# Last products moved into the next phase, and clamps, differences and low weight parts moved from GpSimd to VectorE, in a retention and double feed-forward kernel

## The chip, the cores and the metric

One core of a Trainium2 chip. The metric is the device time of one execution in microseconds, the median of several runs. The program is written with its order by hand: nothing is reordered afterwards, and each engine works through its own instructions in that order.

## The reference

The input passes through a causal retention and then two feed-forward stages, with T = 4608 tokens and a width of 512:

```python
scores = scale * (q @ k.T)                 # 64 (batch, head) pairs of 576 x 64
x = (scores * decay) @ v                   # -> x, 4608 x 512
h = x @ w_in                               # 512 -> 2048
x2 = (h * cos(h)) @ w_out                  # 2048 -> 512
z = max(x2 @ w1, x2 @ w2, x2 @ w3)         # 512 -> 768 each
out = z @ w_out2                           # 768 -> 512
```

All arrays are float32.

## The kernel before

Every large product is made of 2x2 quarters by a scheme with seven products in place of eight (A11, A12, A22, S1 to S4, `P_A11` and so on). Sums and differences of quarters are formed ahead of the products: of the weights in `sums`, of the activations in `difference`, which forms T1 to T4 (T1 and T3 are the two halves of the tile `ta`, T2 and T4 those of `tb`). For precision each operand is split in a high and a low part: ScalarE casts the high part, and VectorE or GpSimd subtracts it from the value to give the low part (`low`, `pair_low`, `piece_low`). One term of a product is three matmuls of 128x128 by 256 columns (low by high, high by high, high by low).

The tokens stand in nine blocks of 512. The program has five phases on TensorE:

1. **A**: the retention of all blocks (units of two heads, `att_unit`) and, beside it, `x @ w_in` for the first half of w_in (tiles `w_wi`, `d_a`, `b_a`, `a_a`, input `x_x`). 18 groups of seven products (`group_in`).
2. **B**: the second half of w_in, with `x_x` read back from memory as `x_y`. 18 groups.
3. **wo**: `g @ w_out` (tiles `w_wo`; the gated `g` is read back as `k_g` and split into `x_g`, `h_g`, `l_g` by `build_out`). 36 groups of seven products (`phase_out`).
4. **b**: the three branches (tiles `w_b`, input `x_z`). 45 groups.
5. **o**: the last product (tiles `w_o`, input `h_m`, `l_m`). 18 groups.

**Slots.** The order is made with an agenda: `at(n, fn)` puts a step n slots ahead, and `tick()` runs the steps that are due. One slot stands for one product, 12 matmuls with two weight pairs. A step that is put late by number of slots is behind those products in every engine's order, not later by a clock.

**The last product of a group.** The product P_A22 of a `group_in` group accumulates onto its bank `d` after S3 has been read from it by VectorE (`plus`, L403). It is held back in `pending` and made by `last_product` (L390) four products into the next group. At the end of phase B and of phase b there is no next group, and `last_product()` stands by itself (L851, L923).

**The gate** h * cos(h) of phases A and B is made per half group by `gate` (L436): ScalarE rounds to whole turns (L441), VectorE forms the rest (L445), GpSimd clamps it (L446), ScalarE takes the cosine (L450), VectorE multiplies (L453), and the result goes to memory.

**Weights.** Outside the phases that need them they are brought to float32 quarters by `background` (widen, join and total; then sums, high and low parts, the low ones on GpSimd by L216) and stored; `take_split` loads the quarters of `wi` 4 to 7 and of `wo`, sums and splits them on VectorE (L190 to L193, L212, L216) just ahead of their use. All `x` tiles share 22 buffers, all weight tiles 8.

The lines that set the order around the change are these:

```python
for i, n in enumerate((-27, -22, -18, -14)):
    at(endA + n, lambda i=i: take_split("wi", 4 + i, 0))
at(offs[0], lambda: difference(o, 1, nc.gpsimd))
at(offs[0], lambda: difference(o, 3, nc.gpsimd))
at(1, turns); at(2, rest); at(4, cosine); at(5, times)
```

Of the kernel before, what the change touches and what calls it, by code (L numbers as in the profile page):

```python
# [101 lines left out]
def retention_ffn(ctx: ExitStack, tc: tile.TileContext, att, w_in, w_out, w123, w_out2, cst, out):  # L102
# [119 lines left out]
    def background(kind, i, arena):  # L222
# [33 lines left out]
        def low(k):  # L256
            piece_low(k, st["src", k], st["p", k], nc.gpsimd)
# [132 lines left out]
    def last_product():  # L390
# [5 lines left out]
        tick()  # L396
# [39 lines left out]
    def gate(s, name, dst):  # L436
# [297 lines left out]
    def build_out(name, n, src, offs, load):  # L734
# [24 lines left out]
        at(offs[0], lambda: difference(o, 1, nc.gpsimd))  # L759
        at(offs[0], lambda: difference(o, 3, nc.gpsimd))  # L760
# [57 lines left out]
    def phase_out(kind, groups, todo, xs, scale, dsts):  # L818
        for j, k in todo:
# [31 lines left out]
    last_product()  # L851

# [128 lines left out]
```

## Time and profile before

| | us |
|---|---|
| median of 3 runs | 1563.21 (1559.2 to 1564.91) |
| the profiled execution's own time | 1566.85 |
| its span from first to last instruction | 1565.0 |
| TensorE busy / VectorE / ScalarE / GpSimd | 1468.8 / 1233.1 / 728.8 / 493.4 |
| mean granted TensorE clock | 0.98 of full |

The shares of the span are 94%, 79%, 47% and 32%. Matmuls are pipelined, so a busy TensorE is not one at its best pace. What counts is how many matmuls a stretch holds beside its length, and what ended the waits within it. An engine's lines give its instructions in groups: how many, busy time in all, mean of one in ns, and the idle time before them with what ended it.

### The profile page before, as it was taken

How to read it: one execution, taken by the hardware profiler on the slowest of the kernel's cores; microseconds unless marked ns; L12 is line 12 of the kernel's file. 1: busy time of each engine (PE TensorE's matmuls, PEld its weight loads, DVE VectorE, ACT ScalarE, POOL GpSimd, SP SyncE). 2: the span in 40 equal slices, each digit the busy share in tenths (PEclk: the TensorE clock that was granted, in tenths of full speed). 3: DMA queues.
4: the chain of work that ended last, by engine and by line, in shares of the span. 5: the costliest groups of instructions: out<-in, count | busy, mean ns of one | idle time of the engine just before them, and what ended most of it. 6: DMA issues, size and time to landing. Idle time of an engine off the chain costs nothing. (4 is left out here: it accounts for less than half of the span.)

```text
span 1565.0 us, 30902 instructions
## 1 busy us (share of the span) xinstructions
PE 1468.8 (94%) x12506; PEld 1424.4 (91%) x12506; DVE 1233.1 (79%) x1611; ACT 728.8 (47%) x1214; POOL 493.4 (32%) x364
## 2 busy tenths in 40 slices
PE   7799999997998996899999999999999999998998
PEld 5698989996988996899999999899999999998998
DVE  6988989898878869899999999746554554538997
ACT  4465655565666665344443444434433333323332
POOL 3544444434333334455444445201110000003221
PEclk9999999997999997999999999999999999999999
DMA  7588888875998873545556656944332211153543
GB/s 287 202 307 316 313 295 301 304 256 212 330 339 303 326 276 132 183 165 177 191 188 209 206 168 253 390 176 142 129 100 83 68 46 50 68 193 137 176 164 133
DMA packets 83086, 324.47 MB, mean 207 GB/s; under 512 B 9216, under 2 KB 9216, under 8 KB 76928
## 3 DMA queue, kind: packets, MB, share of 16 engines
q1 hardware_dynamic: 82944, 322.51, 58.0%
q8 instruction: 98, 1.61, 0.4%
q14 instruction: 44, 0.36, 0.1%
HBM read 190.35 MB, written 132.12 MB: 206 GB/s over the span
## 5 line engine op out<-in xcount | busy, mean ns | idle before, releaser
L781 PE MATMUL wo<-h_g,w_wo 128*128 128x256 f32 x1728 | 317.9, 285 | 0.0
L781 PEld LDWEIGHTS wo<-h_g,w_wo 128*128 128x128 f32 x1728 | 273.0, 194 | 0.0
L781 PE MATMUL wo<-l_g,w_wo 128*128 128x256 f32 x864 | 250.3, 290 | 20.7 <-DVE l_g L754 20.1
L379 PE MATMUL d_b<-x_z,w_b 128*128 128x256 f32 x1944 | 250.1, 284 | 7.0 <-DVE s_b L403 4.9
L379 PEld LDWEIGHTS d_b<-x_z,w_b 128*128 128x128 f32 x1944 | 241.2, 193 | 7.9 <-DVE s_b L403 5.1
L781 PEld LDWEIGHTS wo<-l_g,w_wo 128*128 128x128 f32 x864 | 167.6, 194 | 27.3 <-DVE l_g L754 27.0
L446 POOL TENSOR_SCALAR t_a<-t_a 128x1024 f32<-128x1024 f32 x72 | 91.9, 1281 | 179.9 <-DVE t_a L445 138.2
L379 PE MATMUL d_a<-x_x,w_wi 128*128 128x256 f32 x864 | 126.1, 298 | 9.3 <-DVE x_x L358 7.4
L379 PE MATMUL b_b<-x_z,w_b 128*128 128x256 f32 x972 | 131.9, 284 | 2.0 <-DVE x_z L358 2.0
L379 PE MATMUL d_a<-x_y,w_wi 128*128 128x256 f32 x864 | 116.0, 292 | 18.5 <-DVE s_a L403 7.9
L379 PEld LDWEIGHTS d_a<-x_y,w_wi 128*128 128x128 f32 x864 | 110.5, 199 | 21.6 <-DVE s_a L403 8.1
L379 PEld LDWEIGHTS d_a<-x_x,w_wi 128*128 128x128 f32 x864 | 113.0, 199 | 14.2 <-DVE x_x L358 8.5
L379 PEld LDWEIGHTS b_b<-x_z,w_b 128*128 128x128 f32 x972 | 123.5, 192 | 2.2 <-DVE x_z L358 2.2
L350 POOL TENSOR_TENSOR ta_m<-k_m 128x512 f32<-128x512 f32 (+1 forms) x18 | 18.9, 1048 | 334.0 <-DMA k_m<-mq 273.6
L749 ACT CAST h_g<-tb_g 128x1024 fp32r<-128x1024 f32 x36 | 37.8, 1049 | 179.6 <-DVE tb_g L350 174.1
L781 PE MATMUL o<-h_m,w_o 128*128 128x256 f32 x648 | 117.4, 283 | 0.0
L453 DVE TENSOR_TENSOR s_a<-s_a,t_a 128x1024 f32<-128x1024 f32 x72 | 98.7, 1385 | 15.4 <-ACT t_a L450 15.1
L403 DVE TENSOR_TENSOR s_b<-s_b,b_b 128x512 f32<-128x512 f32 (+1 forms) x45 | 28.5, 634 | 93.7 <-PE b_b L379 92.1
L781 PEld LDWEIGHTS o<-h_m,w_o 128*128 128x128 f32 x648 | 101.1, 192 | 0.0
L445 DVE SCALAR_TENSOR_TENSOR t_a<-s_a,t_a 128x1024 f32<-128x1024 f32 x72 | 97.6, 1375 | 0.4 <-ACT t_a L441 0.4
L450 ACT ACTIVATE t_a<-t_a 128x1024 f32<-128x1024 f32 x72 | 75.7, 1060 | 46.5 <-POOL t_a L446 46.5
L350 POOL TENSOR_TENSOR ta_g<-k_g 128x512 f32<-128x512 f32 x36 | 51.5, 1431 | 128.5 <-DMA k_g<-gq 128.5
(168 smaller groups left out, 3200.0 us busy)
## 6 DMA issues: line engine op xcount, KB each, us to landing
u<-att SPq DMA_DIRECT2D x36, 1024.0 KB, 8.1
gq<-s_a SPq DMA_DIRECT2D x72, 512.0 KB, 6.7
k_g<-gq SPq DMA_DIRECT2D x72, 512.0 KB, 6.6
xs<-x_x SPq DMA_DIRECT2D x63, 512.0 KB, 8.0
x_y<-xs SPq DMA_DIRECT2D x63, 512.0 KB, 7.7
w_b<-st_b SPq DMA_DIRECT2D x8, 1792.0 KB, 14.0
st_b<-p_b SPq DMA_DIRECT2D x27, 512.0 KB, 2.9
raw_b<-w SPq DMA_DIRECT2D x18, 512.0 KB, 5.6
```

Of the source, the lines that this page charges most:

```text
L350: eng.tensor_tensor(out=d, in0=a, in1=b, op=ALU.subtract)
L379: nc.tensor.matmul(h[:, p * HB : (p + 1) * HB], a, b, start=first and p == 0 and i == 0, stop=i == len(terms) - 1, skip_group_check=True,)
L403: nc.vector.tensor_tensor(out=dst, in0=dst, in1=b[:, :n], op=ALU.add)
L445: nc.vector.scalar_tensor_tensor(out=r, in0=s, scalar=INV2PI, in1=st["t"], op0=ALU.mult, op1=ALU.subtract)
L446: nc.gpsimd.tensor_scalar(out=r, in0=r, scalar1=R_MOST, scalar2=R_LEAST, op0=ALU.min, op1=ALU.max)
L450: nc.scalar.activation(r, r, AF.Sin, scale=TURN, bias=HALF_PI)
L453: nc.vector.tensor_tensor(out=s, in0=s, in1=f32(st["t"]), op=ALU.mult)
L749: nc.scalar.copy(h, o[pairs[k][2]])
L781: nc.tensor.matmul(b[:, mt * HB : (mt + 1) * HB], a, v, start=first and mt == 0 and p == 0 and i == 0, stop=last and p == len(ws) - 1 and ...
```

## The change

- `last_product` takes no slot where it is called from `phase_out`: the last products of phases B and b are made ahead of the fifth product of the first group of wo and of o.
- `gate` gets its first slot, a gap and the engine of the clamp. In phase A all is as before; in phase B the clamp is on VectorE, and the steps of the first half stand one slot later.
- `build_out` for wo (`x2_steps`): T1 and T3 on VectorE, T1 one and T3 three slots later, and the cast of `ta` one slot later. For o it is as before.
- `background`: low parts on VectorE; in phase B both halves of a weight are loaded at once, four slots earlier, and converted seven slots after.
- `build_in` of block 0: T1 to T4 on VectorE. The first weight pair is loaded ahead of the first attention inputs, and the first two pairs are converted two slots earlier.
- `take_split` of `wi` 5 to 7 starts 7, 10 and 11 slots later; those of `wo` are moved by a few slots; `load_operands` of the later blocks takes two slots for each load and starts three slots earlier.

```diff
-    def background(kind, i, arena):
+    def background(kind, i, arena, lag=3, both=False):
...
             load_raw(st["raw"], kind, i, 0)
+            if both:
+                load_raw(st["other"], kind, i, 1)
...
-            piece_low(k, st["src", k], st["p", k], nc.gpsimd)
+            piece_low(k, st["src", k], st["p", k], nc.vector)
...
-            at(3 + n, fn)
-        at(6, lambda: load_raw(st["raw"], kind, i, 1))
+            at(lag + n, fn)
+        if not both:
+            at(6, lambda: load_raw(st["raw"], kind, i, 1))
+        second = lag + 2 if both else 9
...
-    def last_product():
+    def last_product(own_slot=True):
...
         g["done"](g, 1)
-        tick()
+        if own_slot:
+            tick()
...
-    def gate(s, name, dst):
+    def gate(s, name, dst, first, gap, eng):
...
-            nc.gpsimd.tensor_scalar(out=r, in0=r, scalar1=R_MOST, scalar2=R_LEAST, op0=ALU.min, op1=ALU.max)
+            eng.tensor_scalar(out=r, in0=r, scalar1=R_MOST, scalar2=R_LEAST, op0=ALU.min, op1=ALU.max)
...
-        at(1, turns)
-        at(2, rest)
-        at(4, cosine)
-        at(5, times)
+        at(first, turns)
+        at(first + 1, rest)
+        at(first + gap, cosine)
+        at(first + gap + 1, times)
...
-    build_in(block_of(0), 9, 13, xsd[0], nc.gpsimd)
+    build_in(block_of(0), 9, 13, xsd[0], nc.vector)
...
-    for i, n in enumerate((-27, -22, -18, -14)):
-        at(endA + n, lambda i=i: take_split("wi", 4 + i, 0))
+    for i, (n, more) in enumerate(((-27, 0), (-15, 0), (-8, 0), (-3, 2))):
+        at(endA + n, lambda i=i, more=more: take_split("wi", 4 + i, more))
...
-        at(endA + per * j + 3, lambda j=j: load_operands(j + 1))
+        at(endA + per * j, lambda j=j: load_operands(j + 1, 2))
         if j < 5:
-            at(endA + per * j + 1, lambda: background(*back.pop(0), True))
-    for i in range(4):
-        at(endA + 5 + 22 * i, lambda i=i: take_split("wo", i, 0))
+            at(endA + per * j - 3, lambda: background(*back.pop(0), True, 7, True))
+    for i, n in enumerate((6, 27, 48, 76)):
+        at(endA + n, lambda i=i: take_split("wo", i, 0))
...
-    for i, n in enumerate((-13, -10, -7, -4)):
-        at(endB + n, lambda i=i, n=n: take_split("wo", 4 + i, 6))
+    for i, (n, more) in enumerate(((-13, 6), (-11, 6), (-9, 11), (-7, 14))):
+        at(endB + n, lambda i=i, more=more: take_split("wo", 4 + i, more))
...
+        late = (1 if half else 2, 3, nc.vector) if k > 1 else (1, 3, nc.gpsimd)
...
-        at(offs[0], lambda: difference(o, 1, nc.gpsimd))
-        at(offs[0], lambda: difference(o, 3, nc.gpsimd))
+        at(offs[t1[0]], lambda: difference(o, 1, t1[1]))
+        at(offs[t3[0]], lambda: difference(o, 3, t3[1]))
...
-        at(offs[3], lambda: pair_high(2))
+        at(offs[last], lambda: pair_high(2))
...
+                if pending and product == P_A22:
+                    last_product(False)
                 product_out(banks[product], ws, product, x, HB * len(ws), first, last)
...
+    x2_steps = {"t1": (1, nc.vector), "t3": (3, nc.vector), "last": 4}
```

How the order of three places changes (a name ends in its block, its group and a running number):

VectorE in phase wo, the operand of block 3, group 2, before. T1 and T3 (`ta`) are on GpSimd and don't stand here:

```order
L745 TENSOR_TENSOR x_g3_2_8308<-k0_g3_2_8244,x_g3_2_8308 128x512
L176 TENSOR_SCALAR spare_167<-spare_167 128x512
L177 SCALAR_TENSOR_TENSOR raw_b3_8263<-raw_b3_8263,spare_167 128x512
L350 TENSOR_TENSOR tb_g3_2_8341<-k1_g3_2_8246,ta_g3_2_8305 128x512
L754 TENSOR_TENSOR l0_g3_2_8343<-k1_g3_2_8246,h0_g3_2_8325 128x1024
L350 TENSOR_TENSOR tb_g3_2_8341<-tb_g3_2_8341,k1_g3_2_8246 128x512
L754 TENSOR_TENSOR l1_g3_2_8380<-tb_g3_2_8341,h1_g3_2_8359 128x1024
L754 TENSOR_TENSOR l2_g3_2_8394<-ta_g3_2_8305,h2_g3_2_8361 128x1024
```

The same with the change:

```order
L356 TENSOR_TENSOR ta_g3_2_8321<-k0_g3_2_8242 128x512
L759 TENSOR_TENSOR x_g3_2_8305<-k0_g3_2_8242,x_g3_2_8305 128x512
L176 TENSOR_SCALAR spare_167<-spare_167 128x512
L177 SCALAR_TENSOR_TENSOR raw_b3_8263<-raw_b3_8263,spare_167 128x512
L356 TENSOR_TENSOR tb_g3_2_8340<-k1_g3_2_8244,ta_g3_2_8321 128x512
L768 TENSOR_TENSOR l0_g3_2_8342<-k1_g3_2_8244,h0_g3_2_8324 128x1024
L356 TENSOR_TENSOR tb_g3_2_8340<-tb_g3_2_8340,k1_g3_2_8244 128x512
L356 TENSOR_TENSOR ta_g3_2_8321<-k1_g3_2_8244,k0_g3_2_8242 128x512
L768 TENSOR_TENSOR l1_g3_2_8380<-tb_g3_2_8340,h1_g3_2_8359 128x1024
L768 TENSOR_TENSOR l2_g3_2_8394<-ta_g3_2_8321,h2_g3_2_8378 128x1024
```

T1 stands first, and T3 between T4 and the low part of `tb`.

ScalarE in phase B, blocks 2 and 3, before (COPY rows empty a bank, `d_a` or `b_a`; L441 and L450 are the gate's turns and cosine):

```order
L411 COPY s0_a3_2_5133<-d_a3_2_5120 128x512
L416 COPY s1_a3_2_5150<-b_a3_2_5137 128x512
L450 ACTIVATE t_a2_2_1_5100<-t_a2_2_1_5100 128x1024
L450 ACTIVATE t_a2_3_0_5118<-t_a2_3_0_5118 128x1024
L423 COPY s0_a3_2_5133<-d_a3_2_5120 128x512
L394 COPY s1_a2_3_5028<-d_a2_3_4995 128x512
```

With the change:

```order
L418 COPY s0_a3_2_5135<-d_a3_2_5122 128x512
L448 ACTIVATE t_a2_3_0_5137<-s0_a2_3_5007 128x1024
L423 COPY s1_a3_2_5152<-b_a3_2_5139 128x512
L457 ACTIVATE t_a2_2_1_5099<-t_a2_2_1_5099 128x1024
L430 COPY s0_a3_2_5135<-d_a3_2_5122 128x512
L457 ACTIVATE t_a2_3_0_5137<-t_a2_3_0_5137 128x1024
L400 COPY s1_a2_3_5029<-d_a2_3_4994 128x512
```

One of the two cosines now stands behind the copy that empties `d_a` after S2.

TensorE at the end of phase B, before: the last product (`x_y8_2`) stands ahead of the first product of wo.

```order
L379 MATMUL d_a8_3_6470<-x_y8_5_6285,w_wi6_4125 128x256 x6
L379 MATMUL d_a8_3_6470<-x_y8_5_6285,w_wi7_4207 128x256 x6
L379 MATMUL d_a8_3_6470<-x_y8_2_6301,w_wi6_4125 128x256 x6
L379 MATMUL d_a8_3_6470<-x_y8_2_6301,w_wi7_4207 128x256 x6
L781 MATMUL wo0_0_6643<-x_g0_0_6533,w_wo0_4563 128x256 x3
```

With the change:

```order
L385 MATMUL d_a8_3_6470<-x_y8_5_6312,w_wi7_4434 128x256 x6
L795 MATMUL wo0_0_6625<-x_g0_0_6531,w_wo0_4578 128x256 x3
...
L795 MATMUL wo0_4_6691<-l1_g0_0_6621,w_wo1_4963 128x256
L385 MATMUL d_a8_3_6470<-x_y8_2_6344,w_wi6_4295 128x256 x6
L385 MATMUL d_a8_3_6470<-x_y8_2_6344,w_wi7_4434 128x256 x6
L795 MATMUL wo0_2_6710<-h1_g0_0_6591,w_wo0_4578 128x256 x2
```

Four products of wo, 48 matmuls, stand between S3 and the last product.

## Rows read from the trace of the kernel before

**Rows 1.** Windows: stretch, length, busy us (instructions) per engine, clock, DMA share, GB/s.

```profile
39.70:91.80 52.10, 42.63 (x405) 38.32 (x403) 46.32 (x79) 27.36 (x58) 25.94 (x21) 0.93 0.64 217
...
351.20:386.10 34.90, 23.31 (x159) 22.61 (x158) 32.32 (x36) 19.28 (x30) 14.40 (x10) 0.79 0.54 201
386.10:505.30 119.20, 108.83 (x854) 106.30 (x854) 93.28 (x111) 76.58 (x112) 42.37 (x32) 0.96 0.91 325
505.30:566.50 61.20, 60.91 (x506) 60.61 (x506) 47.37 (x52) 41.45 (x55) 20.46 (x14) 1.00 0.88 323
566.50:596.10 29.60, 21.73 (x171) 21.45 (x170) 24.65 (x34) 17.48 (x24) 9.81 (x7) 0.89 0.54 194
596.10:651.40 55.30, 44.47 (x338) 43.30 (x338) 51.01 (x54) 27.25 (x41) 29.82 (x19) 0.90 0.42 139
651.40:1000.50 349.10, 332.79 (x2691) 327.18 (x2690) 322.68 (x321) 152.77 (x201) 169.39 (x104) 0.99 0.61 211
...
1050.40:1368.40 318.00, 317.85 (x2649) 317.65 (x2648) 173.12 (x258) 112.86 (x213) 17.90 (x15) 1.00 0.24 84
1368.40:1421.80 53.40, 47.05 (x380) 46.65 (x380) 24.02 (x28) 14.34 (x24) 5.77 (x4) 0.97 0.51 183
```

**Rows 2.** Waits of TensorE from 319 to 606: us in total, times, longest.

```profile
PE d_a L379 <- DVE s_a L403: 7.9, 1, 7.9
PE d_a L379 <- ACT s_a L423: 6.7, 6, 2.0
PE d_a L379 <- DVE x_x L358: 6.6, 2, 6.1
PE d_a L379 <- ACT s_a L411: 5.7, 3, 3.3
PE a_a L379 <- DVE x_x L358: 3.6, 1, 3.6
```

**Rows 3.** Waits of TensorE from 606 to 1000, phase wo.

```profile
PE wo L781 <- DVE l_g L754: 20.1, 13, 2.0
PE wo L781 <- DVE x_g L745: 6.5, 1, 6.5
```

**Rows 4.** Lines of VectorE from 651.4 to 1000.5, phase wo.

```profile
L754 DVE TENSOR_TENSOR l_g<-k_g,h_g 128x1024 fp32r<-128x1024 f32 x32 | 60.2, 1880 | 0.0
L754 DVE TENSOR_TENSOR l_g<-ta_g,h_g 128x1024 fp32r<-128x1024 f32 x32 | 52.7, 1647 | 0.0
L745 DVE TENSOR_TENSOR x_g<-k_g,x_g 128x512 fp32r<-128x512 f32 x31 | 46.6, 1503 | 3.6 <-ACT x_g L741 3.6
L754 DVE TENSOR_TENSOR l_g<-tb_g,h_g 128x1024 fp32r<-128x1024 f32 x32 | 42.5, 1330 | 18.9 <-ACT h_g L749 18.7 <-issue 0.2
L350 DVE TENSOR_TENSOR tb_g<-k_g,ta_g 128x512 f32<-128x512 f32 x32 | 38.6, 1207 | 0.5 <-DMA k_g<-gq 0.5
```

**Rows 5.** Lines of GpSimd in the same stretch.

```profile
L350 POOL TENSOR_TENSOR ta_g<-k_g,k_g 128x512 f32<-128x512 f32 x31 | 60.8, 1963 | 1.9 <-DMA k_g<-gq 1.7
...
L216 POOL TENSOR_TENSOR p_b<-raw_b,p_b 128x512 fp32r<-128x512 f32 x18 | 27.0, 1520 | 0.0
```

**Rows 6.** Lines of VectorE from 1050.4 to 1368.4, phase b.

```profile
L886 DVE TENSOR_TENSOR s_b<-s_b,s_b 128x1024 f32<-128x1024 f32 x35 | 43.3, 1237 | 0.0
...
L358 DVE TENSOR_TENSOR x_z<-k_z,x_z 128x512 fp32r<-128x512 f32 x21 | 14.4, 685 | 3.3 <-ACT x_z L354 3.3
```

**Rows 7.** Waits of ScalarE from 385 to 606, phase B.

```profile
ACT t_a L450 <- POOL t_a L446: 34.5, 26, 3.2
```

**Rows 8.** Lines of VectorE from 386.1 to 505.3, phase B.

```profile
L176 DVE TENSOR_SCALAR ar_wo<-ar_wo 128x512 uint32<-128x512 uint32 x10 | 4.2, 425 | 4.4 <-ACT ar_wo L171 4.4
```

**Rows 9.** Lines of GpSimd in the same stretch.

```profile
L446 POOL TENSOR_SCALAR t_a<-t_a 128x1024 f32<-128x1024 f32 x20 | 28.9, 1451 | 50.0 <-DVE t_a L445 38.4 <-DMA x_y<-xs 5.9 <-issue 5.7
```

**Rows 10.** The DMA view from 960 to 1010.

```profile
DMA packets 3245, 19.45 MB, mean 389 GB/s; under 512 B 363, under 2 KB 363, under 8 KB 2474
```

**Rows 11.** Waits of TensorE from 1000 to 1422, phase b.

```profile
PE d_b L379 <- DVE s_b L403: 4.9, 1, 4.9
```

More of the change, by code (lines that the diff above doesn't have):

```diff
@@ L236, in begin @@
             load_raw(st["raw"], kind, i, 0)
+            if both:
+                load_raw(st["other"], kind, i, 1)
         def convert(n):
+            raw = "other" if both and n else "raw"
             return [
-                lambda: widen(st["raw"], st["t"]),
-                lambda: join(st["raw"], st["t"]),
+                lambda: widen(st[raw], st["t"]),
+                lambda: join(st[raw], st["t"]),
                 lambda: total(
-                    st["raw"], st["fa"][:, 2 * n : 2 * n + 2].rearrange("p q n -> p (q n)"), nc.gpsimd
+                    st[raw], st["fa"][:, 2 * n : 2 * n + 2].rearrange("p q n -> p (q n)"), nc.gpsimd
                 ),
@@ L620, in first_load @@
             load_raw(st["raw"][n], "wi", i, n)
+    first_load(0)
+    att_load(0)
+    att_load(1)
+    first_load(1)
+    att_load(2)
     def first_steps(i):
@@ L712, in load_operands, with build_out @@
         for i, product in enumerate((P_A11, P_S1, P_A12, P_S2, P_S4, P_S3, P_A22)):
-            at(i, lambda product=product: one(product))
+            at(step * i, lambda product=product: one(product))
     later_x = {}
-    at(endA - 7, lambda: load_operands(0))
+    at(endA - 7, lambda: load_operands(0, 1))
     for j in range(NBLK - 1):
-        at(endA + per * j + 3, lambda j=j: load_operands(j + 1))
+        at(endA + per * j, lambda j=j: load_operands(j + 1, 2))
         if j < 5:
-            at(endA + per * j + 1, lambda: background(*back.pop(0), True))
-    for i in range(4):
-        at(endA + 5 + 22 * i, lambda i=i: take_split("wo", i, 0))
+            at(endA + per * j - 3, lambda: background(*back.pop(0), True, 7, True))
+    for i, n in enumerate((6, 27, 48, 76)):
+        at(endA + n, lambda i=i: take_split("wo", i, 0))
     endB = endA + per * NBLK
-    for i, n in enumerate((-13, -10, -7, -4)):
-        at(endB + n, lambda i=i, n=n: take_split("wo", 4 + i, 6))
+    for i, (n, more) in enumerate(((-13, 6), (-11, 6), (-9, 11), (-7, 14))):
+        at(endB + n, lambda i=i, more=more: take_split("wo", 4 + i, more))
     def gate_half(g, half):
         j, k = g["at"]
-        gate(g["s0"] if half == 0 else g["s1"], f"{g['name']}_{half}", gq[j][k][:, 2 * half : 2 * half + 2])
+        late = (1 if half else 2, 3, nc.vector) if k > 1 else (1, 3, nc.gpsimd)
+        gate(g["s0"] if half == 0 else g["s1"], f"{g['name']}_{half}", gq[j][k][:, 2 * half : 2 * half + 2], *late)
     OUT_ORDER = (P_A11, P_A12, P_S4, P_S2, P_A22, P_S3, P_S1)
-    def build_out(name, n, src, offs, load):
+    def build_out(name, n, src, offs, load, t1=(0, nc.gpsimd), t3=(0, nc.gpsimd), last=3):
         o = {"name": name, "n": n}
@@ L849, in retention_ffn @@
                 )
-    last_product()
     todo = [(j, k) for j in range(NBLK) for k in range(4)]
@@ L859, in retention_ffn @@
             lambda j=j, k=k, n=n: outs.__setitem__(
-                (j, k), build_out(f"g{j}_{k}", NB, gq[j][k], range(4, 10) if n else range(2, 8), 0)
+                (j, k), build_out(f"g{j}_{k}", NB, gq[j][k], range(4, 10) if n else range(2, 8), 0, **x2_steps)
             ),
```

21 lines of the change are left out of this document (9 added, 12 removed).

## The prediction

> **What bounds the kernel now.** I read the windows by stage first. In the stretch of phase b from 1050.4 to 1368.4, TensorE makes 2649 matmuls in 318.0 us at clock 1.00 [rows 1]: 0.120 us each, its best pace. A stage's loss is its length less 0.120 us for each of its matmuls. The losses are: end of phase A 34.9 − 159 x 0.120 = 15.8; B blocks 0 to 4 119.2 − 854 x 0.120 = 16.7; B blocks 5 to 7 0.5; the end of B 29.6 − 171 x 0.120 = 9.1 and wo block 0 55.3 − 338 x 0.120 = 14.7, together 23.8 at the boundary; wo blocks 1 to 8 349.1 − 2691 x 0.120 = 26.2; the end of b 7.8 [rows 1]. So TensorE bounds the kernel, and about 90 us are lost in stages that the change touches. Part of each loss is not the wait itself: the granted clock means 0.79 at the end of A and 0.89 and 0.90 at the boundary, against 1.00 in undisturbed stretches [rows 1], so after a long wait some matmuls run at the lower of the two levels (1.2 GHz and not 2.4).
>
> Then the waits of TensorE, stage by stage. At the end of A it waits 3.6 and 6.6 us for parts of `x_x` from VectorE, and at the end of B 7.9 us in one piece for VectorE's `s_a`, which is the last product [rows 2]. In phase B it waits besides 12.4 us for ScalarE to empty a bank [rows 2]. In phase wo it waits 20.1 us in 13 times for `l_g` and 6.5 once for `x_g`, all VectorE [rows 3]. VectorE is busy 322.7 of 349.1 us in wo blocks 1 to 8, and 18.9 us of the rest it waits for ScalarE's `h_g` [rows 1, 4]: there it is VectorE that sets the pace.
>
> Last the lines of VectorE. The same subtraction of 512 columns takes 0.685 us in phase b and one of 1024 takes 1.237, where GpSimd is busy 17.9 of 318 us [rows 1, 6]; in wo, where GpSimd is busy 169.4 of 349 [rows 1], the five long ones of a group take 1.880, 1.647, 1.330, 1.503 and 1.207 [rows 4]. Against 3 x 1.237 + 2 x 0.685 that is an excess of 2.49 us a group.
>
> **T1, T3 and low weight parts on VectorE, phase wo.** GpSimd loses T1 and T3 (T3 alone 1.96 us a group) and low parts, 18 of them in the first form [rows 5]. VectorE gets 2 x 0.685 = 1.37 us a group, and for 26 low parts over 32 groups 26 x 0.685 / 32 = 0.56. If the excess goes, the net is 1.37 + 0.56 − 2.49 = −0.56 us a group, or −18 over 32 groups: 305 busy. T3 also stands where VectorE now idles for `h_g` (0.59 us a group), so it covers most of that idle, and T1 no longer arrives from another engine. A block of four groups then asks some 38 to 40 us of VectorE; TensorE's pace asks 2691 x 0.120 / 8 = 40.4. I keep 6 of the 26.2 us of loss, since the margin is thin: gain 20. Bounds: 25, all waits gone, and 8, if half the excess stays and only the idle is filled. I take the value near the upper end because the rows with a quiet GpSimd are the same operation on the same shapes.
>
> On this excess the Trainium skill ("SBUF — State Buffer", section Who interferes with whom) has a stricter rule: a VectorE instruction with two SBUF inputs and a GpSimd instruction that reads SBUF exclude each other, and the later one waits for the whole of the other. By it all of the time of T1 and T3 on GpSimd would come free for VectorE, and the gain would stand at its upper bound, 25 in place of 20. The durations above agree in sign, but the excess is less than GpSimd's time.
>
> **The clamp on VectorE, B blocks 0 to 4.** ScalarE waits 34.5 us in 26 times of phase B for the clamp on GpSimd [rows 7], and behind its cosine stand the copies that empty TensorE's banks. With the clamp straight behind the `rest` step on the same engine that wait nearly goes. No row has this clamp on VectorE. A one-input operation of 512 columns takes 0.425 [rows 8]; two-input operations grow by 1.237 − 0.685 = 0.55 for 512 more and so have 0.13 fixed, which makes 0.13 + 2 x 0.29 = 0.72. Below is 0.43 (the row as it is), above 1.24, the two-input row of that size [rows 6], or 1.45, what GpSimd takes [rows 9]. I take 0.72, being nearest to a one-input row. VectorE has 93.3 us over five blocks [rows 1], 18.7 each; four clamps add 2.9, and some 0.8 comes back as the multiply and `rest` no longer run beside GpSimd: 20.8 against TensorE's 854 x 0.120 / 5 = 20.5. The third limit is the DMA: 325 GB/s at a share of 0.91 [rows 1] over 23.8 us is 7.75 MB a block, 21.7 us at 325 / 0.91 = 357 GB/s and 19.9 at the highest rate that I see, 389 [rows 10]. I take 21.8 us a block: gain 5 x (23.84 − 21.8) = 10. Bounds 3 (clamp at 1.24) and 16 (no loss). The background loads that come earlier move no bytes more.
>
> **End of A.** The later start of `take_split` takes its sums and low parts from in front of `x_x` on VectorE; both waits go. Next in line are the `x_y` loads, which begin seven slots ahead of the end, and the quarters for `wi` 5 to 7, now closer to their use; all pass through SP's queue. I take half the loss, 8. Bounds 0 (the loads are late by as much) and 14.
>
> **Last products and the boundary from B to wo.** The wait of 7.9 goes: 48 matmuls of wo stand ahead. The gate of that half comes later, but nothing reads its `gq` for many groups. What is late next is VectorE: it is busy 24.7 + 51.0 = 75.7 us in the 84.9 us of these two stretches, where TensorE's pace would ask 509 x 0.120 = 61.1 [rows 1]. From its work go some 2 us (four groups of the excess above), so about 73 us remain, and the stretch can hardly be shorter than that and 2 us of idle: 75, gain 10, with the new wait at the `x_g` of the second group. Bounds: 0, if the work is only late elsewhere, and 18, if the moved `take_split` spreads it into blocks 5 to 7, where VectorE is busy only 47.4 of 61.2 us [rows 1].
>
> **End of b.** The last product waits 4.9 us for VectorE [rows 11]; now it stands behind four products of o. With the clock's part of the loss of 7.8: 5.5, bounds 4 and 6.5.
>
> **Start.** T1 to T4 of block 0 leave GpSimd; at the row of T3 there against VectorE's (1.96 and 0.685 [rows 5, 6]) four of them are 5 us shorter in a chain, of which I count 4, since VectorE is busy 46.3 of 52.1 us in that stretch [rows 1]. The first weight pair goes ahead of the attention inputs in SP's queue: 1.05 MB at 389 GB/s is 2.7 us. Bounds −3 (that delay alone) and +9 (TensorE's idle time, 52.1 − 42.6 [rows 1]).
>
> **Sum.** 4 + 8 + 10 + 10 + 20 + 5.5 = 57.5 us off the profiled execution's 1566.85: 1509.35. That execution lies 3.6 above the median of 1563.21, so on the median's scale 1505.7, given as 1506. The lower bounds add up to 12 and the upper ones to 88.5.
>
> **Rivals.**
> A. VectorE stays the bound of wo. For it: the sum for VectorE holds two additions, 1.93 us a group, against an excess of 2.49 whose cause I infer from GpSimd's busy time. If about half of the excess stays, busy time grows by about 0.7 us a group, 22 us, which eats the idle that T3 fills. The point is 43.6 us (349.1 / 8) of VectorE a block. Against it: the quiet rows. wo and the boundary then gain nothing: 1563.2 − 27.5 = 1536.
> B. The clamp fills VectorE in phase B: at GpSimd's 1.451 [rows 9] a block holds 18.7 + 5.8 − 0.8 = 23.7 us of VectorE, as long as the block now. The gain of 10 falls: 1516. Against it: the 0.425 of 512 columns. The Trainium skill's "GPSIMD Engine Reference", § 4.1 Engine selection, speaks for this rival, as it holds one-input elementwise work on GpSimd to be roughly line-rate; by that the clamp is no shorter on VectorE. No row here shows the two engines at this clamp.
> C. More goes: the terms lie near their upper bounds, less a few us: 1480. For it: nearly all of the loss has a named wait which the change moves.
> D. Slower. VectorE's durations in wo come from something else than GpSimd and don't shrink. T1 and T3 then take 1.503 each, as `x_g` does, and the low parts 26 x 1.207 / 32 = 0.98: 4.0 us a group, 128 in 32 groups, less the idle 349.1 − 322.7 = 26: +101. With the 27.5 gained elsewhere: 1637. It decides once VectorE needs 48 us a block (385 in all); the quiet rows speak against it.
> E. The change does nothing: each loss has a second cause of the same size. 1563.
>
> **How the numbers follow.** Chances: forecast 0.53, A 0.17, B 0.14, C 0.10, D 0.04, E 0.02. The range runs from 1480 (C) to 1540 (A with a smaller gain elsewhere). A measurement of this kernel tells about 0.5% (7.8 us) from no change. Faster by more than that: 0.92; within it 0.03 (E and the worst of A); slower 0.05 (D, and a little for a step that I do not see).
>
> **What the new profile would show.** Right: the long VectorE lines in wo near 1.24 and 0.69 us, blocks of wo near 41 us, the waits for `l_g` nearly gone; ScalarE no longer waiting for the clamp and B blocks 0 to 4 near 21.8; the waits of 7.9 and 4.9 for the last products gone, and at the boundary a wait for the `x_g` of the second group; at the end of A the `x_x` waits replaced by smaller ones for `x_y` or weight loads. Wrong: VectorE lines in wo that stay above 1.5 us, a clamp over 1.2, a boundary as long as now, a start longer than 52 us.

## The result and the profile after

| | before | after |
|---|---|---|
| median, us | 1564.06 (4 runs, 1559.2 to 1569.89) | 1520.99 (4 runs, 1518.4 to 1521.05) |
| ratio of after to before | | 0.971, interval 0.9688 to 0.9733 |
| span of the profiled execution | 1565.0 | 1516.2 |
| TensorE / VectorE / ScalarE / GpSimd busy | 1468.8 / 1233.1 / 728.8 / 493.4 | 1454.9 / 1224.6 / 726.8 / 268.7 |

The kernel is 43 us faster by the medians and 48.8 us by the two spans; the profiled execution of after was the fastest of its four. Forecast were 57.5 us. The windows of after are cut at the same products as the windows of before [rows 1].

Windows of after: stretch, length, busy us (instructions) of TensorE, its weight loads, VectorE, ScalarE and GpSimd, clock, DMA share, GB/s. In order: block 0 of A, the end of A, B blocks 0 to 4, 5 to 7, block 8, wo block 0, wo blocks 1 to 8, the first block of b, and the end of b.

```profile
43.40:94.10 50.70, 43.94 (x405) 39.30 (x403) 43.20 (x79) 27.20 (x58) 21.28 (x18) 0.90 0.63 219
...
353.10:377.40 24.30, 21.05 (x159) 20.44 (x158) 22.80 (x26) 15.67 (x25) 12.22 (x8) 0.93 0.70 271
377.40:494.00 116.60, 107.36 (x855) 106.28 (x854) 107.38 (x140) 80.82 (x118) 28.70 (x18) 0.96 0.93 339
494.00:554.40 60.40, 60.40 (x505) 60.40 (x505) 53.55 (x66) 39.69 (x53) 1.31 (x1) 1.00 0.90 325
554.40:573.20 18.80, 18.80 (x158) 18.77 (x157) 16.63 (x26) 11.82 (x16) 0.00 (x0) 1.00 0.69 249
573.20:634.10 60.90, 48.83 (x351) 46.48 (x350) 59.41 (x78) 33.16 (x50) 10.41 (x6) 0.92 0.42 147
634.10:958.50 324.40, 323.17 (x2689) 322.68 (x2689) 300.79 (x409) 153.24 (x201) 20.25 (x16) 1.00 0.65 225
958.50:1007.20 48.70, 45.90 (x381) 45.49 (x380) 29.09 (x45) 16.00 (x30) 0.00 (x0) 1.00 0.71 276
...
1325.80:1371.50 45.70, 44.15 (x369) 43.95 (x367) 18.39 (x23) 12.35 (x22) 4.25 (x4) 1.00 0.53 191
```

Against [rows 1], read two things in each row: its length, and whether VectorE's busy time is close to it. Wo blocks 1 to 8 are now at TensorE's pace (2689 x 0.120 = 322.7 of 324.4) with VectorE at 300.8. In B blocks 0 to 4 and over B block 8 and wo block 0 together, VectorE is busy 107.4 of 116.6 and 76.0 of 79.7 us.

The waits of TensorE in the same stretches, which answer to [rows 2, 3]: first B blocks 0 to 4, then from block 8 of B to the start of wo block 1, then wo blocks 1 to 8.

```profile
PE d_a L385 <- ACT s_a L418: 5.8, 3, 3.7
PE d_a L385 <- DMA x_y<-xs: 3.3, 1, 3.3
...
PE wo L795 <- DVE l_g L768: 7.0, 6, 1.9
PE wo L795 <- DVE x_g L759: 5.7, 4, 2.6
...
PE wo L795 <- DVE l_g L768: 1.2, 2, 0.7
```

In wo blocks 1 to 8 the waits for `l_g` were 15.8 of the 20.1 us of [rows 3] and are 1.2 now. At the boundary the 7.9 for the last product, 6.5 for `x_g` and 4.3 for `l_g` have become ten shorter waits for `l_g` and `x_g` in wo block 0, 12.7 us together. A transfer, `x_y`, has become a releaser of TensorE in phase B, where none stood in [rows 2].

The lines of VectorE in wo blocks 1 to 8 that answer to [rows 4], with T3 below them:

```profile
L768 DVE TENSOR_TENSOR l_g<-k_g,h_g 128x1024 fp32r<-128x1024 f32 x32 | 45.8, 1430 | 0.3 <-ACT h_g L763 0.3
L768 DVE TENSOR_TENSOR l_g<-tb_g,h_g 128x1024 fp32r<-128x1024 f32 x32 | 39.1, 1222 | 9.2 <-ACT h_g L763 9.2
L768 DVE TENSOR_TENSOR l_g<-ta_g,h_g 128x1024 fp32r<-128x1024 f32 x32 | 39.0, 1219 | 0.0
L759 DVE TENSOR_TENSOR x_g<-k_g,x_g 128x512 fp32r<-128x512 f32 x31 | 26.3, 850 | 0.0
...
L356 DVE TENSOR_TENSOR tb_g<-k_g,ta_g 128x512 f32<-128x512 f32 x32 | 21.9, 685 | 0.0
L356 DVE TENSOR_TENSOR ta_g<-k_g,k_g 128x512 f32<-128x512 f32 x32 | 21.9, 684 | 0.0
```

Three of the five long lines are at 1.22 and 0.685 us, as in the quiet phase b [rows 6]. The other two keep some excess; the only GpSimd work left there is 16 additions.

The clamp on VectorE in B blocks 0 to 4, then in blocks 5 to 7 (its like on GpSimd before: 1.451 [rows 9]):

```profile
L453 DVE TENSOR_SCALAR t_a<-t_a 128x1024 f32<-128x1024 f32 x17 | 17.6, 1034 | 0.6
...
L453 DVE TENSOR_SCALAR t_a<-t_a 128x1024 f32<-128x1024 f32 x12 | 8.3, 694 | 0.4
```

The mean of 1.034 us, in the blocks where GpSimd still adds up the weights of the background, is made of two kinds. This is the same line in blocks 0 to 4, shortest/median/longest in ns, and below it the clamp on GpSimd in the whole kernel before:

```profile
L453 DVE TENSOR_SCALAR t_a<-t_a x17: 693/696/1417, 400.2 to 491.0; 128x1024 f32<-128x1024 f32 x17
...
L446 POOL TENSOR_SCALAR t_a<-t_a x72: 1034/1042/1955, 72.6 to 605.9; 128x1024 f32<-128x1024 f32 x72
```

Nine of the 17 took 0.69 us, and the eight that began while GpSimd was at one of its additions took 1.41 to 1.42. On GpSimd the clamp takes 1.03 us at its shortest and 1.04 in the median.

### The profile page after: what moved, and what is told of

The parts are those of the page before. It is cut to its first block, busy times and chain, and to the rows that moved or that the text cites. A ratio compares the mean times of both kernels' runs of the same rounds, so it can differ in the third digit from the quotient of the medians.

```text
span 1516.2 us, 30767 instructions
## 1 busy us (share of the span) xinstructions
PE 1454.9 (96%) x12506; PEld 1416.0 (93%) x12506; DVE 1224.6 (81%) x1759; ACT 726.8 (48%) x1214; POOL 268.7 (18%) x216
## 4 chain that ended last, share of the span: by engine, by line
PE 46%; DVE 6%; issue 3%; DMA 2%; ACT 1%; POOL 0%; DVEq 0%; SPq 0%; ACTq 0%; POOLq 0%
PE wo L795 17%; PE d_b L385 14%; PE b_b L385 7%; PE o L795 4%; PE a_b L385 3%; DVE l_m L768 1%; DMA st_o<-p_o 1%; DVE tb_m L356 1%; DVE o_o L808 1%; DVE x_m L759 1%; DVE u_o L808 1%; DMA raw_b<-w 1%; DVE l_g L768 0%; DMA k_m<-mq 0%; ACT h_m L763 0%
## 5 line engine op out<-in xcount | busy, mean ns | idle before, releaser
L795 PE MATMUL wo<-l_g,w_wo 128*128 128x256 f32 x864 | 246.6, 285 | 7.6 <-DVE l_g L768 7.6
L460 DVE TENSOR_TENSOR s_a<-s_a,t_a 128x1024 f32<-128x1024 f32 x72 | 90.6, 1274 | 5.9 <-ACT t_a L457 5.9
L410 DVE TENSOR_TENSOR s_b<-s_b,a_b 128x512 f32<-128x512 f32 (+1 forms) x45 | 28.5, 634 | 79.2 <-PE a_b L385 69.4
L795 PE MATMUL o<-l_m,w_o 128*128 128x256 f32 x324 | 91.8, 283 | 0.0
L418 ACT COPY s_b<-d_b 128x512 f32<-128x512 f32 (+1 forms) x45 | 24.5, 544 | 127.3 <-PE d_b L385 120.0
```

The source lines that it names most:

```text
L410: nc.vector.tensor_tensor(out=dst, in0=dst, in1=b[:, :n], op=ALU.add)
L418: nc.scalar.copy(s0[:, 0], d[:, :n])
L460: nc.vector.tensor_tensor(out=s, in0=s, in1=f32(st["t"]), op=ALU.mult)
L795: nc.tensor.matmul(b[:, mt * HB : (mt + 1) * HB], a, v, start=first and mt == 0 and p == 0 and i == 0, stop=last and p == len(ws) - 1 and ...
```

## The experiments

The stages of all runs, in us, cut at the same product of each stage in every run. "Start" is the time of the first product of w_in; "boundary" is block 8 of B and wo block 0 together.

| run | median | start | A 0 | A 1-7 | end of A | B 0-4 | B 5-7 | boundary | wo 1-8 | b 0 | end of b |
|---|---|---|---|---|---|---|---|---|---|---|---|
| before | 1564.06 | 39.7 | 52.1 | 259.4 | 34.9 | 119.2 | 61.2 | 84.9 | 349.1 | 49.9 | 53.4 |
| after | 1520.99 | 43.4 | 50.7 | 259.1 | 24.2 | 116.6 | 60.5 | 79.6 | 324.5 | 48.7 | 45.7 |
| t13_gpsimd | 1546.75 | 43.3 | 50.7 | 259.1 | 24.2 | 117.3 | 60.7 | 85.9 | 346.1 | 50.1 | 45.8 |
| scratch_gpsimd | 1589.27 | 42.3 | 49.1 | 259.1 | 24.2 | 115.5 | 61.7 | 94.6 | 376.9 | 50.1 | 45.7 |
| clamp_gpsimd | 1527.05 | 44.4 | 50.6 | 259.1 | 24.2 | 121.7 | 61.0 | 79.6 | 327.2 | 50.1 | 45.7 |
| loads_early | 1515.26 | 43.3 | 50.6 | 259.1 | 24.2 | 109.0 | 60.5 | 79.6 | 325.7 | 48.7 | 45.7 |
| att_first | 1519.70 | 40.4 | 50.6 | 259.1 | 24.2 | 116.3 | 60.7 | 79.6 | 327.8 | 50.2 | 45.8 |
| b0_gpsimd | 1521.79 | 43.0 | 50.3 | 259.1 | 24.2 | 117.6 | 60.5 | 79.6 | 327.7 | 48.6 | 45.7 |
| own_slot | 1529.67 | 44.3 | 50.6 | 259.1 | 24.3 | 116.3 | 60.5 | 79.6 | 327.8 | 50.2 | 53.5 |
| wi_split_old | 1527.32 | 43.9 | 50.5 | 259.1 | 34.9 | 112.1 | 60.5 | 79.6 | 325.9 | 48.7 | 45.9 |
| low_gpsimd | 1528.46 | 43.2 | 49.1 | 259.1 | 24.2 | 115.4 | 60.5 | 79.6 | 332.2 | 51.0 | 45.8 |
| best1 | 1510.19 | 39.8 | 50.5 | 259.1 | 24.1 | 112.0 | 60.5 | 77.6 | 324.8 | 48.7 | 45.9 |
| best2 | 1508.06 | 40.1 | 50.3 | 259.1 | 24.1 | 111.9 | 60.5 | 75.2 | 325.0 | 50.1 | 46.0 |

Where an edit doesn't touch them, A 1-7, the end of A, the boundary and the end of b repeat within 0.3 us. B 0-4 stands at 115.4 to 117.6, wo 1-8 at 324.5 to 327.8, the first block of b at 48.6 to 50.2, B 5-7 mostly at 60.5, and the start and A 0 each within some 2 us. Smaller differences than these say nothing.

**T1 and T3 back on GpSimd** (ratio to before 0.9875, interval 0.986 to 0.989).

```diff
-    x2_steps = {"t1": (1, nc.vector), "t3": (3, nc.vector), "last": 4}
+    x2_steps = {"t1": (0, nc.gpsimd), "t3": (0, nc.gpsimd), "last": 3}
```

> The changed kernel with T1 and T3 of phase wo back on GpSimd, at their old places, and the cast of ta at its old place; the low weight parts stay on VectorE. Theory (VectorE's instructions are stretched while GpSimd works): the long lines of VectorE in wo go from 1.43, 1.22, 1.22 and 0.85 us back to 1.5 and more for two of them at least, and wo blocks 1 to 8 from 324.4 us to 340 to 350, the whole to 1537 to 1547. Rival (the low parts carried the gain, since they were the larger load of GpSimd per instruction): wo blocks 1 to 8 stay within 5 us of 324.4.

Measured: 21.6 us longer in wo 1-8, 6.3 at the boundary, 1546.75 in all. Two lines of VectorE from 641.1 to 987.2, and that window:

```profile
L768 DVE TENSOR_TENSOR l_g<-ta_g,h_g 128x1024 fp32r<-128x1024 f32 x32 | 49.1, 1533 | 0.0
L759 DVE TENSOR_TENSOR x_g<-k_g,x_g 128x512 fp32r<-128x512 f32 x31 | 43.6, 1407 | 3.5 <-ACT x_g L755 3.5
...
641.10:987.20 346.10, 332.29 (x2690) 328.17 (x2689) 320.07 (x345) 152.59 (x201) 135.58 (x78) 0.99 0.62 213
```

VectorE has 64 instructions fewer (345 against 409, at 0.685 us some 44 us) and is busy 19.3 us longer than in after: its other instructions are stretched by 63 us. Undoing T1 and T3 alone gives back 21.6 of the 24.6 us gained in wo, and all of the boundary's gain. The shares don't simply add up: undoing the low parts alone gives back several us of wo too (below).

**Work on GpSimd that nothing waits for** (1.015, 1.0133 to 1.0167: 1.5% longer than before).

```diff
             nc.scalar.copy(x[:, 0], o["k1"][:, 0])
+            if name[0] == "g":
+                for _ in range(2):
+                    nc.gpsimd.tensor_tensor(out=cs[:, :NB], in0=cs[:, :NB], in1=cs[:, NB : 2 * NB], op=ALU.subtract)
```

> The changed kernel, with two subtractions of 512 columns more on GpSimd for each group of phase wo, on constants that nothing reads any more; nothing waits for them and no other engine's order changes. Theory (work on GpSimd stretches VectorE's instructions): the five long lines of VectorE in wo gain 1.5 to 2.5 us a group together, VectorE asks 300.8 + 32 x 2 = 365 us, and wo blocks 1 to 8 go from 324.4 to 345 to 370 us. Rival (the stretching before came from what waits for what, or from transfers): these lines stay within 3% and the stage within 2 us of 324.4.

Measured: wo 1-8 take 376.9 us, VectorE is busy 361.3. The theory's 365 for VectorE comes near; its upper end of 370 for the stage is exceeded by 7. The boundary, whose operands get the same extra work, is 15.0 us longer. Timeline of GpSimd around 770 us, then of VectorE (start us, duration us; x6 is six in a row):

```profile
769.46 1.37 POOL L183 TENSOR_TENSOR fa_b<-raw_b 128x512 uint32<-128x512 uint32 x1 [4.20 <-DVE raw_b L177]
770.78 10.44 POOL L758 TENSOR_TENSOR cs<-cs 128x512 f32<-128x512 f32 x6
```

```profile
769.84 1.53 DVE L762 TENSOR_TENSOR x_g<-k_g,x_g 128x512 fp32r<-128x512 f32 x1
771.29 1.77 DVE L356 TENSOR_TENSOR tb_g<-k_g,ta_g 128x512 f32<-128x512 f32 x1
772.99 2.31 DVE L771 TENSOR_TENSOR l_g<-k_g,h_g 128x1024 fp32r<-128x1024 f32 x1
775.22 1.77 DVE L356 TENSOR_TENSOR tb_g<-tb_g,k_g 128x512 f32<-128x512 f32 x1
...
786.51 0.68 DVE L356 TENSOR_TENSOR ta_g<-k_g 128x512 f32<-128x512 f32 x1
787.12 0.68 DVE L762 TENSOR_TENSOR x_g<-k_g,x_g 128x512 fp32r<-128x512 f32 x1
```

T2 and T4 (`tb`), subtractions of 512 columns, take 0.68 us with GpSimd idle and 1.77 while the six run. Of the 32 instances of T3 in the stage, 17 took 0.68 to 0.69 us, and the 15 that began while GpSimd was at work took 1.78 to 1.79, with nothing in between. Of all the operand lines of VectorE in the stage, the 60 instructions that began while GpSimd was at work were stretched, and none of the other 192. The rival, that waits or transfers stretched them, is out: no data depends on these instructions, and they move none by DMA.

**The clamp of phase B back on GpSimd** (0.9749, 0.9735 to 0.9764).

```diff
-        late = (1 if half else 2, 3, nc.vector) if k > 1 else (1, 3, nc.gpsimd)
+        late = (1 if half else 2, 3, nc.gpsimd) if k > 1 else (1, 3, nc.gpsimd)
```

> The changed kernel with the clamp of phase B back on GpSimd, at its new slots. Theory (the clamp on VectorE, though mis-sized beside the background work, saves ScalarE's wait): B blocks 0 to 4 go from 116.6 to 120 or more and blocks 5 to 7 stay near 60.4. Rival (late loads set the pace of blocks 0 to 4, whoever makes the clamp): 116.6 within 1.5 us. A third (VectorE is full in blocks 0 to 4, at 107.4 of 116.6 us, and the clamp's 1.03 us each is what fills it): 113 or less.

Measured: B 0-4 121.7 us, 5.1 longer; B 5-7 61.0. Its lines in blocks 0 to 4, of VectorE and then of GpSimd:

```profile
L460 DVE TENSOR_TENSOR s_a<-s_a,t_a 128x1024 f32<-128x1024 f32 x20 | 30.5, 1525 | 8.2 <-ACT t_a L457 8.0
...
L453 POOL TENSOR_SCALAR t_a<-t_a 128x1024 f32<-128x1024 f32 x20 | 25.5, 1284 | 50.6 <-DVE t_a L452 28.0 <-issue 9.9 <-PE d_a L385 7.6
```

The theory holds: the clamp on VectorE is worth 5 us there, and neither rival (within 1.5 us of 116.6; 113 or less) came out. It asks 17.6 us of VectorE, but the multiply alone goes back from 1.525 to 1.217 us, and VectorE's busy time differs by only 4 us (103.3 and 107.4).

**Two kinds of loads earlier** (0.9673, 0.9655 to 0.9691).

```diff
-        at(endA + n, lambda i=i: take_split("wo", i, 0))
+        at(endA + n - 5, lambda i=i: take_split("wo", i, 0, 5))
...
-    at(endA - 7, lambda: load_operands(0, 1))
+    at(endA - 9, lambda: load_operands(0, 1))
```

The fourth argument of `take_split`, added here, puts its sums, high and low parts so many slots later after its load.

> The changed kernel with the loads of w_out's quarters in phase B issued five slots earlier, their conversion where it was, and the first block's operands of phase B loaded two slots earlier. Theory (two late loads, waits of 3.3 us of TensorE for x_y and 4.1 us of VectorE for the quarters, and the lower clock after them cost B blocks 0 to 4 most of their remaining loss): 353.1 to 494.0, now 140.9 us, gets 6 to 10 us shorter. Rival (the DMA engines, at a share of 0.93, are full): the waits turn up at other loads and the stretch gets less than 2 us shorter. Rival (VectorE is full there): at most 3 us shorter, with VectorE busy over 95% of it.

Measured: the end of A and B 0-4 together take 133.2 in place of 140.8 us: 7.6 shorter, as the theory had it. Window of B 0-4:

```profile
377.30:486.20 108.90, 103.72 (x853) 102.50 (x853) 106.41 (x140) 80.42 (x118) 31.86 (x18) 1.00 0.98 358
```

The clock is 1.00 (0.96 in after), and now both rivals' limits are reached at once: VectorE 106.4 of 108.9 us, the DMA engines at 0.98 and 358 GB/s. What was late in after is seen in SP's queue at the end of A (start, us of the issues):

```profile
368.78 1.80 SPq L720 DMA_DIRECT2D x_y<-xs  x3
375.59 0.32 SPq L466 DMA_DIRECT2D gq<-s_a  x1
376.00 0.38 SPq L720 DMA_DIRECT2D x_y<-xs  x1
...
380.54 3.13 SPq L720 DMA_DIRECT2D x_y<-xs  x4
```

and, among SP's own waits from 365 to 392:

```profile
SPq L466 <- DVE s_a L460: 7.1, 2, 4.9
```

A store of a gate's result waits 4.9 us for its data from VectorE, and the four loads of block 0's `x_y` that stand behind it wait with it. In block 2, VectorE waited for a quarter of w_out:

```profile
438.67 0.42 DVE L190 TENSOR_TENSOR s_wo<-fa_wo 128x256 f32<-128x256 f32 x1 [4.08 <-DMA fa_wo<-wf_wo]
```

Behind this sum stood the additions of `s_a`, and behind those the copies that free TensorE's bank: a sum that stood too soon behind its load held all three engines. Block by block, B 0-4 of after takes 26.9, 21.2, 26.6, 20.2 and 21.7 us: the two blocks with a late load are the long ones. Here it is 24.5, 21.0, 21.7, 20.2 and 21.6.

**The start as it was** (0.9684, 0.9664 to 0.9705).

```diff
+    att_load(0)
+    att_load(1)
     nc.tensor.matmul(state, cs[:, :CH], cs[:, :NB], start=True, stop=True, skip_group_check=True)
...
-    first_load(0)
-    att_load(0)
-    att_load(1)
-    first_load(1)
-    att_load(2)
...
+    first_load(0)
+    att_load(2)
+    first_load(1)
...
-    lead_in(0, 0)
-    at(2, lambda: lead_in(1, 0))
...
-    for i, n in ((2, 12), (3, 15)):
+    for i, n in ((0, 2), (1, 4), (2, 12), (3, 15)):
```

> The changed kernel with the start as it was: the first attention inputs are loaded ahead of the first weight pair, and its two first pairs are converted two slots later; T1 to T4 of block 0 stay on VectorE. Theory (the weight pair in front of the attention inputs costs what the inputs come later, and the earlier conversion gives nothing back): the first product of w_in comes at 39.7 and not 43.4 us, block 0 stays near 50.7, the whole 3 to 4 us shorter. Rival (the earlier conversion is what shortened block 0 by 1.4 us): block 0 back at 52, the whole 1 to 2 us shorter or the same.

Measured: the first product 3.0 us earlier than in after and 1.9 earlier than in any other run that keeps the changed start; block 0 unchanged. The whole is 1.3 us shorter where 3 to 4 were expected. In the profiled execution wo 1-8 and b 0 were 3.3 and 1.5 longer; the sign of the total can't be told from noise, that of the stage can.

**T1 to T4 of block 0 on GpSimd** (0.970, 0.968 to 0.972).

```diff
-    build_in(block_of(0), 9, 13, xsd[0], nc.vector)
+    build_in(block_of(0), 9, 13, xsd[0], nc.gpsimd)
```

> The changed kernel with T1 to T4 of block 0 back on GpSimd. Theory (GpSimd's chain of four differences at 1.3 to 1.8 us held the parts that TensorE waits for in block 0): block 0 gets 3 to 5 us longer than 50.7. Rival (TensorE waits there for ScalarE's state copies, whoever forms the differences): within 1.5 us.

Measured: block 0 50.3 against 50.7 us. The rival holds: in this block TensorE waits for ScalarE (7.3 us for `state` and `u` in this run, 5.7 in after), and the differences were worth nothing. What shortened block 0 from 52.1 stays open; undoing either of the two parts leaves it short, both at once weren't tried.

**Last products in slots of their own** (0.9747, 0.9722 to 0.9772).

```diff
-                if pending and product == P_A22:
-                    last_product(False)
...
+    last_product()
     todo = [(j, k) for j in range(NBLK) for k in range(4)]
...
+    last_product()
     todo = [(j, k) for j in range(NBLK) for k in range(2)]
```

> The changed kernel with the last products of phases B and b in slots of their own, ahead of the next phase. Theory (the wait for the last product at the end of B only covered part of what VectorE has to do before the second group of wo, so that little was won there): the stretch from block 8 of B to the end of wo block 0, now 79.7 us, gets 0 to 3 us longer, with a wait of several us for VectorE's s_a in it and shorter waits for x_g; at the end of b, where VectorE is idle half the time, the full 5 to 7.5 us are lost. Rival (the last product was worth its whole wait at both places): 8 us longer at the first.

Measured: the boundary takes 79.6 us either way; the end of b 7.8 us longer. Waits of TensorE from 540 to 650, and from 1360 to 1410:

```profile
PE d_a L385 <- DVE s_a L410: 8.5, 1, 8.5
PE wo L795 <- DVE l_g L768: 3.7, 6, 0.9
PE wo L795 <- DVE x_g L759: 3.1, 1, 3.1
...
PE d_b L385 <- DVE s_b L410: 4.9, 1, 4.9
```

At the boundary the wait of 8.5 us only takes the place of others: VectorE's work ends at the same time. At the end of b, where VectorE is busy less than half of the time, the move gives its wait and the clock's share. Of the 7.8 us, 1.4 only change their stage: with the move, the 12 matmuls of the last product are made in phase o, behind the cut. The window of own_slot holds 381 matmuls, that of after 369:

```profile
1332.40:1385.90 53.50, 47.07 (x381) 46.67 (x380) 24.03 (x28) 14.35 (x24) 5.77 (x4) 0.96 0.50 182
```

**The splitting of w_in's quarters at its old slots** (0.9735, 0.9717 to 0.9754).

```diff
-    for i, (n, more) in enumerate(((-27, 0), (-15, 0), (-8, 0), (-3, 2))):
+    for i, (n, more) in enumerate(((-27, 0), (-22, 0), (-18, 0), (-14, 0))):
```

> The changed kernel with the splitting of w_in's quarters 5 to 7 at its old slots. Theory (this alone made the gain at the end of A): 353.1 to 377.4, now 24.3 us, gets 9 to 12 us longer, with x_x late on VectorE again, and block 0 of B up to 4 us shorter since its operands' loads have no weight load in front. Rival (the rest of the program's end of A, such as the later gate, did it): less than 4 us longer.

Measured: the end of A 10.7 us longer, at the 34.9 of before, and B 0-4 4.5 shorter (block 0 of B 23.0 and not 26.9). The later splitting alone made the gain at the end of A, and gave four of it back through the late `x_y`.

**Low parts of the background on GpSimd** (0.975, 0.9734 to 0.9767).

```diff
-            piece_low(k, st["src", k], st["p", k], nc.vector)
+            piece_low(k, st["src", k], st["p", k], nc.gpsimd)
```

> The changed kernel with the low parts of the background weights (w_b, in phase wo and in the first blocks of b) back on GpSimd, T1 and T3 on VectorE. Theory (work on GpSimd stretches VectorE's lines by about the time of VectorE's own share of it or more): the 26 low parts cost VectorE 26 x 0.69 = 18 us less and stretch other lines by 10 to 25 us, so wo blocks 1 to 8 stay within 6 us of the 324 to 328 that the changed kernel and its variants show. Rival (the low parts on GpSimd carry most of the stretching that the change took away): 335 or more.

Measured: wo 1-8 332.2 us, 7.7 longer than in after and 4.4 above the longest of the unchanged variants: within the theory's 6 us of 324 to 328, and short of the rival's 335. VectorE is busy 307.9 us there with 24 instructions less, so the others are stretched by 7 + 24 x 0.685 = 23.5 us.

**Two versions put together** (0.9641, 0.9628 to 0.9654; and 0.9626, 0.9613 to 0.9639). Both take the edits of loads_early and att_first, and besides:

```diff
-nc.gpsimd if k == 2 else nc.vector)
+nc.gpsimd if k == 2 and (kind, i) not in plain else nc.vector)
```

> The changed kernel with the earlier loads of the run loads_early, the start of the run att_first, and the low parts that the splitting of quarters still gave to GpSimd on VectorE. Theory (GpSimd's work stretches VectorE's by more than it takes away): wo block 0 goes from 60.9 to 58 to 60 us though VectorE gets four more low parts, B blocks 0 to 4 from 108.9 to 107 to 109, and the whole to 1506 to 1513. Rival (these low parts are simply more work for a VectorE that is full there): wo block 0 at 62 to 64 us, the whole 1512 to 1518.

The second one also has:

```diff
-    for i, (n, more) in enumerate(((-13, 6), (-11, 6), (-9, 11), (-7, 14))):
+    for i, (n, more, ahead) in enumerate(((-23, 14, 2), (-21, 14, 2), (-9, 11, 0), (-7, 14, 0))):
```

> The same, with the quarters of the fifth and sixth pair of w_out loaded ten and added up eight slots earlier, in block 7 of B, where VectorE has time left; their high and low parts stay where they were. Theory (the stretch from block 8 of B to the end of wo block 0 is as long as VectorE's work in it): 3.4 us of sums leave it and it gets 2 to 4 us shorter. Rival (the longer held buffers make other loads late): blocks 5 to 7 of B or block 8 get longer by as much or more.

The boundary in best1, then in best2:

```profile
546.00:623.60 77.60, 66.71 (x507) 64.99 (x506) 73.95 (x107) 45.12 (x65) 2.64 (x2) 0.93 0.50 173
...
546.10:621.30 75.20, 65.30 (x506) 63.59 (x505) 72.93 (x104) 45.10 (x65) 2.65 (x2) 0.95 0.50 171
```

In best1 VectorE makes four more low parts at the boundary and is busy 2.1 us less (76.04 in after), and the stretch is 2.0 us shorter, as the theory had it. In B 0-4 the same edit missed: 112.0, where loads_early had 109.0 and 107 to 109 were expected, with VectorE busy 109.5 and not 106.4; there five low parts moved and were simply more work, or it is within the spread of that stage. So the 7.6 us of the earlier loads rest on the one profiled execution of loads_early, whose median is 5.7 us under that of after; with these low parts beside them B 0-4 is 4.6 us shorter than in after. In best2 the stretch gets 2.4 us shorter, and blocks 5 to 7 don't get longer. At 1508.06 best2 is the fastest of all, 59 us under the kernel before of its own comparison, where the change itself is 43 under that of its own.

## Why the prediction was right in direction, and 15 us too low

The measured 1521 lies inside 1480 to 1540; the likeliest value was 1506. By its steps, from the table of stages:

| step | forecast gain | measured |
|---|---|---|
| start and block 0 | 4 | −2.3 |
| end of A | 8 | 10.7 |
| B blocks 0 to 4 | 10 | 2.6 |
| boundary | 10 | 5.3 |
| wo blocks 1 to 8 | 20 | 24.6 |
| end of b | 5.5 | 7.7 |

The stages sum to 48.6 where 57.5 were forecast (1.4 of the 7.7 at the end of b have only moved into phase o, see below); 48.45 is also the difference of the two profiled executions' own times (1566.85 and 1518.4). The medians are 43 apart, so 5 of the 15 us come from the two executions and not from the steps. The steps miss in both directions: wo and the end of A gave 7.3 us more than forecast, the start, B and the boundary 18.4 less. That the sum lies well inside the range is in part their cancelling.

**wo: right in mechanism, low in size.** The excess of 2.49 us a group was read rightly as GpSimd's doing, and rival D, which doubted that, is excluded by the run with scratch work. VectorE came out at 300.8, where 305 were reckoned, and no wait of size is left, so the gain reached its upper bound of 25. That was the value by the Trainium skill's "SBUF — State Buffer", section Who interferes with whom: two exclusive instructions, the later one waiting for the whole of the other. The runs agree with it as far as they go: T3 took 0.68 or 1.78 us in the scratch run, by whether it began while GpSimd was at work. My objection, that the excess was less than GpSimd's time, weighed a sum over instructions of which only some meet. The same section exempts a VectorE instruction with at most one input from SBUF, outside certain modes. In wo blocks 1 to 8 of before, 25 additions that read a TensorE bank and one tensor began while GpSimd was at work and took 0.684 us on average, and the other 31 took 0.683. Most are of this line (shortest/median/longest in ns):

```profile
L794 DVE SCALAR_TENSOR_TENSOR o_wo<-wo,u_wo x32: 682/688/692, 656.5 to 999.7; 128x512 f32<-128x512 f32 x32
```

The clamp also reads one tensor and is stretched all the same; whether it runs in one of those modes no run shows.

**B blocks 0 to 4: the step that failed.** The clamp was priced at 0.72 and takes 0.694 alone, but the prediction put that price beside a GpSimd that still adds up weights in these blocks: it is 1.03 there on average. It is worth 5.1 us (clamp_gpsimd). What was lost went to two late loads, 7.6 us (loads_early); the three blocks without one took 21.2, 20.2 and 21.7 us, below the 21.8 that was forecast. Rival B's outcome, a gain in B that falls away, thus nearly came, but not by its cause. The sentence that the earlier background loads move no bytes more was true and beside the point: the change also moves single loads behind others in SP's queue, and the prediction named that only at the end of A. Of rival B, the Trainium skill's "GPSIMD Engine Reference", § 4.1 Engine selection, would have the clamp no slower on GpSimd; its median on GpSimd is 1.04 us in the kernel before, and alone on VectorE it takes 0.694, so the runs speak against that for this instruction. (The 12.4 us of waits for ScalarE that the prediction put into phase B hold 1.9 of the end of A.)

**End of A: right, and partly repaid.** The `x_x` waits shrank from 9.7 us to 2.3; what came next was `x_y`, as named, but it came in block 0 of B and so in the next stage's account: 10.7 gained, 4.5 given back.

**Boundary: the right bound, with the wrong load.** The forecast said that the stretch can't be shorter than VectorE's work in it and 2 us. That holds (76.0 of 79.7 us, and best1 and best2 shorten it by taking work out). But the work was put at 73 us, and it didn't fall: nine T1 and T3 (6.1 us), two low parts (1.4) and seven clamps of phase B (4.9), which the sum left out, add 12.4 us, and the other lines get shorter by only about as much. What fell is VectorE's idle time, from 9.2 to 3.7 us. And the prediction credited the last product, which is worth nothing here (own_slot); the 5.3 us hang on T1 and T3 (t13_gpsimd gives back 6.3).

**End of b: right.** Without the 1.4 us that moved into phase o (144.7 us, where it was 143.2) the stage gains 6.3, inside the bounds of 4 to 6.5; own_slot gives back 6.4 by the same count.

**Start: wrong sign.** The 2.7 us for the weight pair in front was named as a bound and should have been a term: it costs some 3 us (3.0 by att_first). The 4 us for the differences of block 0 were argued from GpSimd's longer instructions alone, without a row in which TensorE waits for them; with them undone, b0_gpsimd is no longer in that block.

Rivals A, C and E fell with the stages: VectorE isn't the bound of wo any more, and the terms were not all near their upper ends.

## What to carry to other kernels

Before an instruction is given to another engine, look at what it does to the third instruction that runs beside it: here two subtractions moved *onto* the busiest engine made that engine's total shorter, and this can be read beforehand as the same line at two durations in two phases. Where one engine's busy time fills a stretch (76.0 of 79.7 us at the boundary), taking away another engine's wait inside it gained nothing; taking work out of it did (best1, best2). The change itself gained there by cutting that engine's own idle time (9.2 us before, 3.7 after). When loads are put later to save buffers, follow the queue that issues them: one store that waits for its data holds all the loads behind it, and the cost appears a stage later.

## What was not expected of the hardware

In the run with scratch work the stretching goes by whether GpSimd had begun before: T3 takes 0.68 or 1.78 us, `x_g` 0.68 or 1.53, and the low part of `k_g` 1.22 or 2.06 to 2.31. The stretched length is not the same everywhere: in wo blocks 1 to 8 of before, where GpSimd does several kinds of work, `x_g` took 0.68 us (5 times), 1.24 to 1.37 (6) or 1.77 to 1.79 (20). And it reaches an instruction that reads one tensor from SBUF: the clamp took 0.69 or 1.41 us, the latter each time that GpSimd was at an addition when it began.
